# Splitting every second weight unit again in each batch, with its sign word from GpSimd and the last attention spread out

## The chip, the cores and the metric

The kernel runs on one core of one Trainium2 chip. The metric is device time in microseconds (us) of one execution. Five engines work side by side, each through its own queue in order: TensorE (PE, with its weight loads as PEld), VectorE (DVE), ScalarE (ACT), GpSimd (POOL) and SyncE (SP, which issues nearly all DMAs here).

## The reference

Attention with a soft cap, then a gated feed-forward layer, for 4 batches of 448 tokens, 12 heads of 64, a width of 768 and a hidden width of 1536:

```
scores = q k^T / sqrt(64);  scores = cap * tanh(scores / cap);  attn = softmax(scores);  a = attn v
x = a, laid out as [4*448, 768]
out = (sigmoid(x w_gate) * (x w_val)) w_out
```

q, k and v are float32. The three weight matrices are float64.

## The kernel before, in words

**Two streams on TensorE.** The attention works on 24 pairs of heads, six pairs to a batch. The feed-forward part, `moe(b)`, works on batch b. Both are Python generators, and the loop at the end of `_emit` weaves them: while `moe(b)` runs, the attention of batch b + 1 is issued in between. Each yields the size of the step it has issued, in TensorE terms, and the loop (L981) takes the attention's next step whenever `done_a * tot_m <= done_m * tot_a`, with `tot_m` 545 and `tot_a` = 12 x `o.head(b + 1)`. The instructions of TensorE and ScalarE keep the order in which they are issued here. The order of VectorE, GpSimd and SyncE is set by a planner when the kernel is built, from expected costs and from priorities (`high_priority`). [...]

**The feed-forward part.** The weights are cut into 36 units of 128 x 768: 24 for gate and value (an even unit and the odd one behind it belong together), 12 for the output. Each float32 operand is split into a high part (`o.hi`, a copy into fp32r) and a low part (`o.lo`, the difference), and each product is three fp32r matmuls: 18 of them by 448 columns for a gate or value unit (L836), 18 of 384 columns for an output unit in batches 0 to 2 (L927). A batch yields 24 x 18 = 432 steps for gate and value, and 12 x 3 x 5.14 = 185 for the output, 617 in all.

**The weights in batch 0.** A unit comes as 64-bit words into `w64` (three buffers). `convert_w` makes float32 words of it in one of two slots of `pair0`: ScalarE scales the upper words (L728), VectorE shifts them left by 3 (L729), ors in the sign bit of the upper word (L730), and adds the rounded lower word (L731). `split_w` splits the float32 unit into a tile of the pool `w` (four buffers), by ScalarE and VectorE (GpSimd for the first four units, which are converted before the feed-forward part begins). The split unit, 768 KB, is stored to DRAM (`store_w`, L777). `next_w(u)` converts up to unit u + 4, splits unit u + 3 and loads up to unit u + 3. The batches 1 to 3 load every unit split (`load_to`, L787).

**The attention of the pairs 12 to 23** (batches 2 and 3) splits its probabilities too. For a pair n and a head j: scores and tanh, exp, `emit_P` (ScalarE makes `ph`, VectorE `pl`; one buffer each), `emit_PV` (seven matmuls into the one PSUM bank `pv`, L459 to L461), `emit_rd` (ScalarE copies half of `pv` to `tmp`, L486, and VectorE adds it into `xraw`, L488, which frees `pv`). `emit_out` divides by the sum, and `x_done` splits the result into `xspl`. `emit_PV(n - 1, ...)` is issued in iteration n, between the scores of pair n. Iteration 24 has no scores of its own (`live` is false): only both `emit_PV` of pair 23 and its end are left.

Of the kernel before, what the change touches and what calls it, by code (L numbers as in the profile page):

```python
# [9 lines left out]
F32 = mybir.dt.float32  # L10
# [6 lines left out]
ALU = mybir.AluOpType  # L17
AX = mybir.AxisListType

P = 128  # L20
# [228 lines left out]
def _bounded_attention(o, x_done):  # L249
# [14 lines left out]
    nc, c, ap = o.nc, o.c, o.ap  # L264
# [3 lines left out]
    B, H, S, D, NF, NC, R = o.B, o.H, o.S, o.D, o.NF, o.NC, o.REST  # L268
# [6 lines left out]
    def direct(n):  # L275
        return n < DIRECT

    def alone(n):

        return n < o.NPAIR  # L280
# [3 lines left out]
    def held(n):  # L284

        return n < o.NPAIR - 1
# [6 lines left out]

        return 3 * AHEAD_OF if n == o.NPAIR - 1 else AHEAD_OF

    o.head = lambda b: 25 if direct(b * o.NPAIR) else 18.5


    fill = o.ps_m.tile([P, P], F32, tag="m", name="fill")
# [1 line left out]
    def keep_busy(n):  # L301

        for _ in range(n):
            nc.tensor.matmul(fill, ident, ident, start=True, stop=True)
# [97 lines left out]
    def emit_P(n, j):  # L402

        t = Pt[n][:, j]
        ph = ap.tile([P, NC, S], F32R, tag="ph", bufs=1, name=f"ph{n}_{j}")
        pl = ap.tile([P, NF, S], F32R, tag="pl", bufs=1, name=f"pl{n}_{j}")
        o.hi("a", ph, t)
        o.lo("v", pl, t[:, 0:NF, :], ph[:, 0:NF, :])
        o.lo("v", ph[R:P, NF, :], t[R:P, NF, :], ph[R:P, NF, :])
        Phl[n, j] = (ph, pl)  # L410
        a = ap.tile([P, S], F32, tag="a", bufs=1, name=f"a{n}_{j}")
        nc.gpsimd.tensor_add(a, t[:, 0, :], t[:, 1, :])  # L412
        nc.gpsimd.tensor_add(a, a, t[:, 2, :])
        nc.gpsimd.tensor_add(a[0:R], a[0:R], t[0:R, NF, :])
        f = a[0:D]
        nc.vector.tensor_add(f, f, a[D:P])
        s = ap.tile([P, S], F32R, tag="as", bufs=2, name=f"as{n}_{j}")
        o.hi("p", s[0:D], f)
        o.lo("v", s[D:P], f, s[0:D])
        Asum[n, j] = s  # L420
# [9 lines left out]
    def emit_R(n):  # L430

        for j in range(2):
            rows = half(j)
            nc.tensor.matmul(
                new_pv(n, j), vs[n][rows, NF, :], Pt[n][rows, 0, NF, :], start=True, stop=False
            )
# [89 lines left out]
    for n in range(NP + 1):  # L526
        live, last = n < NP, n == o.NPAIR
        if live:
            due = emit_S(n, 0) + emit_S(n, 1)
            if n in PLAN:  # L530
                o.convert_to(PLAN[n])
            yield due
        if n == 0:
            keep_busy(3)
        if n > 0:
            if packed(n - 1):
                emit_R(n - 1)
                yield 4
            yield from emit_PV(n - 1, 0)
            if not held(n - 1):  # L540
                emit_rd(n - 1, 0)
            if not direct(n - 1):
                emit_P(n - 1, 1)
        first = n == o.NPAIR
        if first:
            yield from emit_PV(n - 1, 1)
            emit_rd(n - 1, 1)
            emit_out(n - 1)
        if live:
            if packed(n):  # L550
                yield emit_S(n, 3) + emit_S(n, 2)
            else:
                yield emit_S(n, 2) + emit_S(n, 3)
            if n == 0:
                keep_busy(3)
            emit_T(n + 1)
            if n == 0:
                keep_busy(8)
            if 0 < n and n + 2 < NP:
                qks[n + 2] = o.load_qk(n + 2, direct(n + 2), packed(n + 2))  # L560
            yield 5
            if first:
                yield None
            emit_exp(n, 0)
            if not direct(n):
                emit_P(n, 0)
        if n > 0:
            if not first:
                yield from emit_PV(n - 1, 1)
                if alone(n - 1):  # L570
                    emit_rd(n - 1, 0)
                emit_rd(n - 1, 1)
                emit_out(n - 1)
                yield 2
            vs.pop(n - 1)
            if n % o.NPAIR == 0 and not first:
                yield None
            load_v(n + 1)
        if not live:
            return  # L580
        emit_exp(n, 1)
        split_v(n + 1)
# [84 lines left out]
def _emit(tc, ctx, c, attention_of, q, k, v, w_gate, w_val, w_out, out):  # L667
    nc = tc.nc
    B, H, S, D = q.shape
# [7 lines left out]
    WRAW = 2  # L677
    KEEP = 4
    AHEAD = 3
    WB = 4  # L680
    CLOSE = 3

    big = ctx.enter_context(tc.tile_pool(name="big", bufs=1))
    wp = ctx.enter_context(tc.tile_pool(name="wp", bufs=2))
    dram = ctx.enter_context(tc.tile_pool(name="dram", bufs=1, space=bass.MemoryType.DRAM))
    ps_m = ctx.enter_context(tc.tile_pool(name="ps_m", bufs=3, space=bass.MemoryType.PSUM))
    o = _Ops(tc, ctx, c, q, k, v)
# [7 lines left out]
    UN = KD * P  # L695
    NU = 3 * KF
# [7 lines left out]
            src.append(wt[:, x:x + KU])  # L704
    w_dram = {}
    w_raw = {}
    w_in = {}

    def load_w64(u):
# [4 lines left out]
    def convert_w(u):  # L714

        words = w_in.pop(u).bitcast(I32).rearrange("p (n t) -> p n t", t=2)
        low, top = words[:, :, 0], words[:, :, 1]
        at = conv["next"] % WRAW * UN
        x = c["pair0"][:, at:at + UN]
        xi = x.bitcast(I32)
        half = x.bitcast(U16).rearrange("p (n t) -> p n t", t=2)[:, :, 0]
        nc.scalar.activation(x, top.bitcast(F32), AF.Copy, scale=2.0 ** -112)  # L728
        nc.vector.tensor_scalar(xi, xi, 3, None, ALU.logical_shift_left)  # L729
        nc.vector.scalar_tensor_tensor(xi, top, -2 ** 31, xi, ALU.bitwise_and, ALU.bitwise_or)  # L730
        nc.vector.scalar_tensor_tensor(  # L731
            half, low.bitcast(U32), 2.0 ** -29, half, ALU.mult, ALU.add
        )
        w_raw[u] = x
        if u < o.early:
            split_w(u)

# [24 lines left out]
    def split_w(u):  # L762

        if u not in w_raw:
            return
        t, s = w_raw.pop(u), new_w(u)
        o.hi("p" if u < o.early else "a", s[:, 0, :], t)
        o.lo("p" if u < o.early else "v", s[:, 1, :], t, s[:, 0, :])
        if u < KEEP or u >= o.early:
            w_spl[u] = s  # L770
        if not u < KEEP:
            store_w(u, s)

    def store_w(u, s, queue=nc.sync):
# [1 line left out]
        w_dram[u] = d  # L776
        queue.dma_start(out=d.bitcast(F32), in_=s.bitcast(F32))  # L777

    loaded = {"next": 0}

    def load_to(n):
        while loaded["next"] < min(n, B * NU):
            u = loaded["next"]
            loaded["next"] += 1
            if KEEP <= u < o.early or NU <= u:
                t = new_w(u)
                nc.sync.dma_start(out=t.bitcast(F32), in_=w_dram[u % NU].bitcast(F32))  # L787
                w_spl[u] = t
# [24 lines left out]
    LEAD = 5  # L813
# [5 lines left out]
    def next_w(u):  # L819
        if u < NU:  # L820
            convert_to(u + LEAD)
        split_w(u + AHEAD)
        load_to(u + WB)
        w = w_spl.pop(u)
        if u < KEEP:
            store_w(u, w, nc.scalar)
        return w

    def moe(b):
# [75 lines left out]
        for t in range(2):  # L905
# [6 lines left out]
            end = b == B - 1 and t == 1  # L912
            by_chunk = KF - CLOSE * KU if end else KF
            x = 0
# [53 lines left out]
    with tc.manual_schedule(engines=MS):  # L968
# [4 lines left out]
        for b in range(B):  # L973
# [6 lines left out]
            while live_m or live_a:  # L980
                if live_a and (not live_m or done_a * tot_m <= done_m * tot_a):  # L981
                    n = next(att, None)
# [4 lines left out]
                else:  # L987
                    n = next(m, None)
# [34 lines left out]
```

## Time and profile before

| | |
|---|---|
| median of 3 runs | 759.17 us (758.65 to 760.04) |
| the profiled execution | 758.98 us |
| its span, first to last instruction | 757.2 us |
| PE busy | 742.8 us (98%) |
| PEld, DVE, ACT, POOL busy | 642.5, 467.4, 349.4, 202.3 us |
| granted TensorE clock, mean | 0.999 |
| DMA | 170.63 MB, mean 225 GB/s |

Busy times are sums over the whole span. The kernel has stages with different loads (attention alone, batch 0 with the conversions, batches 1 and 2 with attention, batch 3 without), so shares of the whole span say little of any one of them. A wait of an engine costs time only if the end hangs on that engine.

### The profile page before, as it was taken

What the parts mean: (1) busy time and instruction counts of PE and PEld (TensorE: products, weight loads), DVE (VectorE), ACT (ScalarE), POOL (GpSimd) and SP (SyncE); (2) the same over time, 40 slices, a digit from 0 to 9 for tenths busy, and PEclk for the clock granted to TensorE, in tenths of its full rate; (3) what the DMA queues carried; (4) which work ended last, traced back from release to release, by engine and by line L of the source; (5) the groups of instructions that cost most, each with busy time, mean ns of one, the idle gap of its engine ahead of it and who ended that gap; (6) DMA issues with size and microseconds to landing.
All of it is one profiled execution on the core that took longest, in us unless ns stands there. A gap on an engine that the chain in (4) does not pass through costs nothing.

```text
span 757.2 us, 10267 instructions
## 1 busy us (share of the span) xinstructions
PE 742.8 (98%) x3922; PEld 642.5 (85%) x3922; DVE 467.4 (62%) x503; ACT 349.4 (46%) x383; POOL 202.3 (27%) x223
## 2 busy tenths in 40 slices
PE   8999999999999999999999999999999999999997
PEld 7555878777778888988899988888889999999996
DVE  2698789979998938878786628878785011111000
ACT  5888577667576445555554245555540000000000
POOL 1354000021210516363535306353551000000000
PEclk9999999999999999999999999999999999999999
DMA  4867899999999866555677956644589866665541
GB/s 100 222 161 156 284 346 360 330 307 302 285 267 376 298 212 196 179 186 178 183 222 232 288 185 193 199 143 158 166 234 313 273 223 226 226 225 180 176 168 56
DMA packets 133509, 170.63 MB, mean 225 GB/s; under 512 B 86860, under 2 KB 111948, under 8 KB 133452
## 3 DMA queue, kind: packets, MB, share of 16 engines
q1 hardware_dynamic: 131788, 166.44, 69.8%
q10 hardware_dynamic: 1664, 3.46, 1.3%
q8 instruction: 33, 0.54, 0.3%
q14 instruction: 24, 0.20, 0.1%
HBM read 132.91 MB, written 36.18 MB: 223 GB/s over the span
## 4 chain that ended last, share of the span: by engine, by line
PE 78%; DVE 10%; DMA 3%; SPq 2%; issue 2%; POOL 2%; ACT 2%; DVEq 0%; POOLq 0%; ACTq 0%
PE h L836 43%; PE o L927 18%; PE sc L389 5%; PE pv L450 4%; DVE rd L506 2%; PE pv L459 2%; PE pv L460 2%; DVE pl L213 1%; PE tp L242 1%; DMA v<-in_v_dram 1%; PE pv L441 1%; DVE pair L731 1%; PE tp L350 1%; DVE pair L730 1%; DVE wspl L213 1%
## 5 line engine op out<-in xcount | busy, mean ns | idle before, releaser
L836 PE MATMUL h<-xspl,wspl 128*128 128x448 f32 x1728 | 377.4, 372 | 0.3 <-DVE osb L949 0.3
L836 PEld LDWEIGHTS h<-xspl,wspl 128*128 128x128 f32 x1728 | 321.3, 188 | 42.4 <-issue 15.5
L927 PE MATMUL o<-wspl,gspl 128*128 128x384 f32 x864 | 159.3, 338 | 0.2 <-DVE osb L949 0.2
L927 PEld LDWEIGHTS o<-wspl,gspl 128*128 128x128 f32 x864 | 150.5, 188 | 4.8 <-issue 3.8
L392 ACT ACTIVATE t<-sc,scale 128x896 f32<-128x896 f32 (+1 forms) x90 | 85.9, 1002 | 43.9 <-PE sc L389 43.7
L205 POOL TENSOR_SCALAR gspl<-gate 128x448 fp32r<-128x448 f32 x48 | 35.9, 748 | 251.7 <-DVE gate L880 251.7
L877 ACT ACTIVATE gate<-h 128x448 f32<-128x448 f32 x48 | 26.0, 541 | 161.3 <-PE h L836 159.8
L400 ACT ACTIVATE t<-t,capv 128x1792 f32<-128x1792 f32 (+2 forms) x48 | 83.2, 1738 | 0.1
L880 DVE SCALAR_TENSOR_TENSOR gate<-gate,h 128x448 f32<-128x448 f32 x48 | 29.7, 618 | 77.1 <-PE h L836 72.1
L506 DVE RECIPROCAL rd<-rd 128x448 f32<-128x448 f32 x24 | 70.7, 2946 | 5.3 <-ACT rd L479 3.1
L389 PE MATMUL sc<-T 64*128 64x448 f32 (+1 forms) x540 | 69.1, 382 | 1.9 <-DVE T L213 1.7
L389 PEld LDWEIGHTS sc<-T 64*128 64x128 f32 (+1 forms) x540 | 46.4, 181 | 22.3 <-issue 10.9
L949 DVE TENSOR_SCALAR osb<-o 128x384 f32<-128x384 f32 x22 | 12.0, 553 | 73.1 <-PE o L927 73.0
L412 POOL TENSOR_TENSOR a<-t 128x448 f32<-128x448 f32 x24 | 31.6, 1315 | 84.8 <-ACT t L400 46.9
L213 DVE TENSOR_TENSOR gspl<-gate,gspl 128x448 fp32r<-128x448 f32 x48 | 36.6, 763 | 22.3 <-POOL gspl L205 22.1
L207 ACT ACTIVATE ph<-t 128x1792 fp32r<-128x1792 f32 x24 | 40.7, 1696 | 16.4 <-PE pv L461 10.1
L213 DVE TENSOR_TENSOR pl<-t,ph 128x1344 fp32r<-128x1344 f32 x24 | 45.6, 1899 | 2.4 <-ACT ph L207 1.9
L213 DVE TENSOR_TENSOR T<-tp,T 128x960 fp32r<-128x960 f32 (+1 forms) x24 | 27.3, 1136 | 27.8 <-ACT T L207 27.8
L731 DVE SCALAR_TENSOR_TENSOR pair<-w,pair 128x768 uint16<-128x768 uint32 x36 | 41.7, 1162 | 0.3
L728 ACT ACTIVATE pair<-w 128x768 f32<-128x768 f32 x36 | 32.5, 904 | 18.9 <-DVE wspl L213 7.2
L450 PE MATMUL pv<-t,vo 112*128 112x448 f32 x96 | 40.1, 539 | 0.4 <-ACT t L400 0.4
L730 DVE SCALAR_TENSOR_TENSOR pair<-w,pair 128x768 int32<-128x768 int32 x36 | 35.5, 990 | 0.6
(81 smaller groups left out, 716.3 us busy)
## 6 DMA issues: line engine op xcount, KB each, us to landing
wspl<-wd SPq DMA_DIRECT2D x108, 768.0 KB, 4.4
wd<-wspl SPq DMA_DIRECT2D x32, 768.0 KB, 6.3
w<-in_moe_w_gate_dram SPq DMA_DIRECT2D x12, 768.0 KB, 6.7
w<-in_moe_w_val_dram SPq DMA_DIRECT2D x12, 768.0 KB, 7.0
w<-in_moe_w_out_dram SPq DMA_DIRECT2D x12, 768.0 KB, 7.1
qk<-in_q_dram SPq DMA_DIRECT2D x46, 112.0 KB, 4.1
out_dram<-osb SPq DMA_DIRECT2D x24, 192.0 KB, 3.3
qk<-in_k_dram SPq DMA_DIRECT2D x34, 96.0 KB, 2.7
```

The lines of the kernel that those rows point to most:

```text
L205: self.nc.gpsimd.tensor_scalar(dst, src, 1.0, 1.0, ALU.mult, ALU.mult)
L207: self.nc.scalar.activation(dst, src, AF.Copy)
L213: e.tensor_sub(dst, src, hi.bitcast(F32))
L389: nc.tensor.matmul(ps[0:w, j, 0:S], a[rows], r[rows], start=(i == 0), stop=(i == len(ops) - 1))
L392: nc.scalar.activation(Pt[n][0:w, :, m, :], ps[0:w, :, 0:S], AF.Tanh, scale=c["scale"][0:w])
L400: nc.scalar.activation(t, t, AF.Exp, scale=c["cap"][rows])
L450: nc.tensor.matmul(pv, vs[n][0:QC, j * NC + m, :], Pt[n][0:QC, j, m, :], start=(m == 0), stop=(m == NC - 1),)
L506: nc.vector.reciprocal(rd, rd)
L730: nc.vector.scalar_tensor_tensor(xi, top, -2 ** 31, xi, ALU.bitwise_and, ALU.bitwise_or)
L731: nc.vector.scalar_tensor_tensor(half, low.bitcast(U32), 2.0 ** -29, half, ALU.mult, ALU.add)
L836: nc.tensor.matmul(ps, a, r, start=(kk == 0 and i == 0), stop=(kk == KD - 1 and i == 2))
L927: nc.tensor.matmul(ps, a, r, start=(y + kk == 0 and i == 0), stop=(y + kk == KF - 1 and i == 2),)
```

## The change

Three things change.

**Sign word.** In `convert_w`, GpSimd multiplies the upper words by 0.0 in place, which leaves a word with the sign bit alone. One VectorE instruction then shifts and ors. L729 goes, L730 changes its form, and each conversion has a GpSimd instruction between ScalarE and VectorE.

**Units stored unsplit.** Of the units 4 to 27 the odd ones (12 of them) are stored as float32, 384 KB, straight from the slot of `pair0`, and not as split tiles. In the batches 1 to 3 they are loaded into the two slots of `pair0` by `load_raw_to`, up to unit u + 6 in `next_w(u)`, and `split_w` splits unit u + 3 by ScalarE and VectorE.

**The last attention.** `o.head` of batch 3 is 17.8 in place of 18.5, and iteration 24 yields 5 steps ahead of each of its two `emit_PV`.

```
-    o.head = lambda b: 25 if direct(b * o.NPAIR) else 18.5
+    o.head = lambda b: 25 if direct(b * o.NPAIR) else 17.8 if b == B - 1 else 18.5
...
+        if not live:
+            yield 5
         if n > 0:
             if packed(n - 1):
...
+        if not live:
+            yield 5
         if n > 0:
             if not first:
                 yield from emit_PV(n - 1, 1)
...
+    WHOLE = 28
...
+    def whole(u):
+        u %= NU
+        return u % 2 == 1 and KEEP <= u < WHOLE and o.early == KEEP
...
         nc.scalar.activation(x, top.bitcast(F32), AF.Copy, scale=2.0 ** -112)
-        nc.vector.tensor_scalar(xi, xi, 3, None, ALU.logical_shift_left)
-        nc.vector.scalar_tensor_tensor(xi, top, -2 ** 31, xi, ALU.bitwise_and, ALU.bitwise_or)
+        sign = top.bitcast(F32)
+        nc.gpsimd.tensor_scalar(sign, sign, 0.0, None, ALU.mult)
+        nc.vector.scalar_tensor_tensor(xi, xi, 3, top, ALU.logical_shift_left, ALU.bitwise_or)
...
         w_raw[u] = x
+        if whole(u):
+            d = dram.tile([P, UN], F32, name=f"wr{u}")
+            w_dram[u] = d
+            nc.sync.dma_start(out=d, in_=x)
...
-        if not u < KEEP:
+        if KEEP <= u < NU and not whole(u):
             store_w(u, s)
...
+    def load_raw_to(n):
+        while loaded["raw"] < min(n, B * NU):
+            u = loaded["raw"]
+            loaded["raw"] += 1
+            if NU <= u and whole(u):
+                at = loaded["slot"] % WRAW * UN
+                loaded["slot"] += 1
+                x = c["pair0"][:, at:at + UN]
+                nc.sync.dma_start(out=x, in_=w_dram[u % NU])
+                w_raw[u] = x
...
-            if KEEP <= u < o.early or NU <= u:
+            if KEEP <= u < o.early or NU <= u and not whole(u):
...
         load_to(u + WB)
+        load_raw_to(u + LEAD + 2)
```

## Rows read from the trace of the kernel before

**Rows 1.** Windows: the stretch, its length, busy us (instructions) by engine, clock, DMA.

```profile
120.00:140.00 20.00, 20.00 (x98) 16.00 (x97) 17.59 (x24) 13.35 (x17) 1.66 (x3) 1.00 1.07 361
...
480.00:500.00 20.00, 20.00 (x108) 17.49 (x107) 18.00 (x17) 11.74 (x13) 10.88 (x11) 1.00 0.56 181
...
560.00:580.00 20.00, 17.54 (x96) 16.64 (x95) 16.30 (x17) 5.44 (x6) 7.54 (x7) 1.00 0.93 258
```

**Rows 2.** Waits of PE, whole span: us in total, times, longest.

```profile
PE sc L389 <- DVE T L213: 1.7, 4, 0.7
```

**Rows 3.** Timeline of PE, in batch 0, then iteration 24: start, us, what, [idle before <- releaser].

```profile
214.57 0.66 PE L350 MATMUL tp<-ident,qk 128*128 128x128 f32 x4 [0.90 <-ACT t L392]
...
556.67 3.29 PE L927 MATMUL o<-wspl,gspl 128*128 128x384 f32 x18
...
562.40 0.44 PE L459 MATMUL pv<-pl,vs 128*128 128x448 f32 x1 [0.99 <-DVE xraw L488]
...
563.90 3.31 PE L927 MATMUL o<-wspl,gspl 128*128 128x384 f32 x18
568.69 0.47 PE L459 MATMUL pv<-pl,vs 128*128 128x448 f32 x1 [1.48 <-DVE pl L213]
```

**Rows 4.** The chain that ended last, behind iteration 24: start, us, what.

```profile
573.93 26.01 PE o L927 x150
```

**Rows 5.** Timeline of DVE, iteration 24.

```profile
561.64 0.61 DVE L488 TENSOR_TENSOR xraw<-pv,tmp 64x448 f32<-64x448 f32 x1
...
567.09 1.54 DVE L213 TENSOR_TENSOR pl<-t,ph 128x1344 fp32r<-128x1344 f32 x1
...
579.65 0.61 DVE L213 TENSOR_TENSOR xspl<-xraw,xspl 128x448 fp32r<-128x448 f32 x1
```

**Rows 6.** Groups by line: shapes xcount | busy us, mean ns | idle before.

```profile
L730 DVE SCALAR_TENSOR_TENSOR pair<-w,pair 128x768 int32<-128x768 int32 x36 | 35.5, 990 | 0.6
...
L213 DVE TENSOR_TENSOR wspl<-pair,wspl 128x768 fp32r<-128x768 f32 x32 | 32.8, 1024 | 0.7 <-ACT wspl L207 0.6
...
L207 ACT ACTIVATE wspl<-pair 128x768 fp32r<-128x768 f32 x32 | 27.0, 843 | 18.9 <-PE h L836 11.2 <-PE o L927 4.3 <-DVE pair L731 1.8
...
L729 DVE TENSOR_SCALAR pair<-pair 128x768 int32<-128x768 int32 x36 | 21.5, 596 | 14.6 <-ACT pair L728 14.5
...
L205 POOL TENSOR_SCALAR wspl<-pair 128x768 fp32r<-128x768 f32 x4 | 3.3, 832 | 4.0 <-DVE pair L731 4.0
```

**Rows 7.** Timeline of POOL ahead of batch 0: beside a conversion, and without one.

```profile
50.67 0.93 POOL L205 TENSOR_SCALAR xspl<-xraw 128x448 fp32r<-128x448 f32 x1 [3.26 <-DVE xraw L510]
51.68 1.71 POOL L213 TENSOR_TENSOR xspl<-xraw,xspl 128x448 fp32r<-128x448 f32 x1
...
70.78 1.13 POOL L213 TENSOR_TENSOR xspl<-xraw,xspl 128x448 fp32r<-128x448 f32 x1
```

**Rows 8.** Timeline of DVE, a tight place while batch 2's feed-forward runs.

```profile
473.67 1.54 DVE L213 TENSOR_TENSOR pl<-t,ph 128x1344 fp32r<-128x1344 f32 x1
```

**Rows 9.** PE's use of that tile.

```profile
478.16 0.36 PE L459 MATMUL pv<-pl,vs 128*128 128x448 f32 x1
```

**Rows 10.** DVE and its slot of `pair0` in batch 0.

```profile
127.00 1.05 DVE L731 SCALAR_TENSOR_TENSOR pair<-w,pair 128x768 uint16<-128x768 uint32 x1
```

**Rows 11.** ACT in batch 0: the slot's next use; a held split.

```profile
134.43 0.89 ACT L728 ACTIVATE pair<-w 128x768 f32<-128x768 f32 x1
...
211.65 0.85 ACT L207 ACTIVATE wspl<-pair 128x768 fp32r<-128x768 f32 x1 [3.03 <-PE o L927]
```

**Rows 12.** DMA issues: xcount, KB each, median us to landing.

```profile
wd<-wspl SPq DMA_DIRECT2D x32, 768.0 KB, 6.3
```

**Rows 13.** Timeline of DVE in the conversion of rows 7.

```profile
51.21 1.19 DVE L730 SCALAR_TENSOR_TENSOR pair<-w,pair 128x768 int32<-128x768 int32 x1
52.44 1.88 DVE L731 SCALAR_TENSOR_TENSOR pair<-w,pair 128x768 uint16<-128x768 uint32 x1
54.19 1.16 DVE L213 TENSOR_TENSOR T<-tp,T 128x960 fp32r<-128x960 f32 x1
```

More of the change, by code (lines that the diff above doesn't have):

```diff
@@ L777, in store_w @@
         queue.dma_start(out=d.bitcast(F32), in_=s.bitcast(F32))
-    loaded = {"next": 0}
+    loaded = {"next": 0, "raw": 0, "slot": 0}
+    def load_raw_to(n):
[8 more added lines that the diff above has]
+                w_raw[u] = x
     def load_to(n):
```

## The prediction, made before the changed kernel had run

> **What bounds the kernel now.** I read the busy time in stretches first, then PE's waits, then the timelines around each wait. In the stretches [rows 1] the reader sees a kernel bound by TensorE: in batch 0 (the first row) and while batch 2's feed-forward runs (the second) PE is busy for 20.00 of 20 us. An engine that gets less work there, or a queue that moves fewer bytes, gives nothing back by itself. One stretch late in the run falls short, 560 to 580 us with 17.54 busy: 2.46 us are missing. Two smaller places come from PE's waits: 1.7 us in four waits of scores for the low half of `T`, made by DVE, ahead of batch 0 [rows 2], and 0.90 us of a transpose for a tanh of ACT, at 214.57 in batch 0's output part [rows 3]. So the change can win at most about 2.5 + 1.7 + 0.9 us, unless it makes matmuls faster, which it doesn't touch.
>
> The hole is iteration 24, where the last pair has no scores left to stand between its two `emit_PV` [rows 3]. The first PV matmul at 562.40 has waited 0.99 us for `xraw` (L488 frees the bank `pv`), and that of the second head at 568.69 has waited 1.48 us for `pl`.
>
> **The spread of the last attention.** The two waits fall if the steps put between fill them. With the new `tot_a` of 12 x 17.8 = 213.6, five attention steps stand against 5 x 545 / 213.6 = 12.8 feed-forward steps, 2.5 chunks of 5.14, so two or three chunks. A chunk is six matmuls, 1.04 us by the chain's 150 in 26.01 us [rows 4]. So each yield puts 2.1 to 3.1 us of other TensorE work ahead of a PV.
>
> First wait: from the end of the previous PV (556.67, where the next matmuls start) to the end of L488 at 561.64 + 0.61 = 562.25 [rows 3, 5] are 5.6 us. The order left 562.40 - 0.99 - 556.67 = 4.7 us of work between; now 6.8 to 7.8. The wait goes, with at least 1.2 us to spare. Second wait: from 563.90 to the end of `pl` at 567.09 + 1.54 = 568.63 are 4.7 us, and 3.3 us of work stood between [rows 3, 5]; now 5.4 to 6.4, so at least 0.7 us to spare. Both together give 2.47 us.
>
> What is late next? The attention of batch 3 ends later, and batch 3 must find its `xspl`. Before, the attention's yields in this loop (five pairs of 37 steps and 16 at the end) came to 201 of 222, which ends it at 201 / 222 x 545 = 493 of the 617 feed-forward steps; now 211 of 213.6, at 538. That leaves (617 - 538) / 185 x 216 = 92 matmuls, 16 us by the same chain, in place of 26. The work behind the last yield is a normalization and a split of one row block, which ended at 580.26 [rows 5], 6.3 us into those 26 (they begin at 573.93). So some 10 us of cover are left. The last wspl splits of batch 3's units that `next_w` issues in the output part are those of units 25 and 27, issued with units 22 and 24, before iteration 24; none falls into it.
>
> **The sign word.** Per conversion DVE loses L729, 0.596 us, and the merged instruction should cost what L730 does, 0.990 (it has the same two inputs) [rows 6]. Over 36 units DVE gets 21.5 us less. GpSimd gets 36 instructions; the trace has none on every second word, so I bound them: nothing below, since it could hide fully, 0.83 us for a copy of as many packed words [rows 6], and 1.71 us, a subtraction beside a busy DVE [rows 7]. I take 0.83, the same count of elements, 30 us in all, in a stretch where GpSimd is busy 1.66 of 20 us [rows 1]. The chain of a conversion grows by 0.83 - 0.60 = 0.2 us. In batch 0 that is hidden twice: DVE's own time, and a lead of four units; if the cover were gone, it would cost 36 x 0.2 = 7 us at most. DVE's 21.5 us cover nothing that PE waits for, so they give zero, but for the 0.9 us and 1.7 us above, which I leave at zero: there the instruction that falls away is replaced by one that must be waited for.
>
> **Units stored unsplit.** Stores of 12 units shrink from 768 to 384 KB, and so do 36 loads: 48 x 0.384 MiB = 18 MiB less of 170.63 MB. PE waited for none of these loads, so this gives zero. In each later batch ACT gets 12 x 0.843 = 10.1 us and DVE 12 x 1.024 = 12.3 us [rows 6]. Two waits are new. On ACT the split of a unit waits for its load and for a buffer that TensorE frees with the unit before the current one; behind it stand the tanh and exp that are issued during the current unit, and TensorE reaches those no earlier. On SP a raw load waits until the slot's former unit is split, and behind it stand the loads of split units; these are issued three units ahead of their use, at least 3 x 3.3 us of output matmuls [rows 3], and a delay of some 3 us is covered. In batch 3 ACT and DVE are nearly idle. In batches 1 and 2 DVE is at up to 18.00 of 20 us [rows 1]; a whole unit comes every two units, some 10 us, so two a stretch, 2.0 us: 20.0. That is full in this stretch, so the slack decides. The tightest place of the PV chain is `pl`, ready at 473.67 + 1.54 = 475.21 and used at 478.16 [rows 8, 9], 2.95 us; three more of the 24 places are within 0.3 us of it. One split put into that chain delays it by 0.84 + 1.02 = 1.9 us, less than 2.95. I take zero; two splits at each of the four places would cost about 4 x (3.7 - 2.95) = 3 us, a split slowed by GpSimd to 1.8 us as many as four.
>
> The raw store holds the slot that the conversion two units later needs. In batch 0, L731 ends at 128.05 [rows 10] and the slot is used again at 134.43 [rows 11]: 6.4 us. A 768 KB store lands 6.3 us after its issue [rows 12]; half of it should land between 3.2 and 6.3. Unless SP's queue adds much, it fits, and I take zero.
>
> **Sum.** 758.98 (profiled) - 2.47 = 756.5. The median of the runs shown is 0.2 above the profiled execution, so 756.7.
>
> **Rivals.**
>
> *A wait in place of the one removed, no change.* The second PV has 0.7 us to spare only, and the pace of the whole last attention shifts by 4%. If DVE's order in iteration 24 puts 2 us of other work ahead of `pl`, most of the second wait comes back: 758.2 with all of it. Against it: the PV comes 2 us later, and the other work that stood there does not. With small delays elsewhere this is 757.7 to 760.6.
>
> *Held slots, slower.* SP's queue works in order; a raw store behind loads that wait can land later than 134.43. Then L728 stands at the head of ACT, and behind it the tanh that frees the score banks. The price is in the trace: a split that held ACT for 3.03 us, to 211.65 [rows 11], stands ahead of the tanh for which PE waited 0.90 us [rows 3]. Half of the 12 stores late by that much cost 6 x 0.9 = 5.4 us: 762.1. It decides from three such holds, which eat the gain; five make it slower.
>
> *GpSimd ahead of batch 0, slower.* There the low half of `T` stands behind the conversion on DVE, and PE waits for it. GpSimd begins the two instructions of a split of `xspl` at 50.67 [rows 7], beside the conversion. If the planner puts the sign word behind both, it starts at 53.4 and ends at 54.2, where the split of `T` now begins [rows 13], and the two VectorE instructions of the conversion come behind it: 0.99 to 1.19 and 1.05 to 1.88 [rows 6, 10, 13], 2.0 to 3.1 us. As DVE would stand idle meanwhile, the subtraction on GpSimd would take 1.13 in place of 1.71 [rows 7], so 1.4 to 3.1 us, in four conversions: 5.6 to 12.4 us, 762.3 to 769.1. It decides from a delay of 1 us each. Against it: GpSimd had stood idle for 3.26 us before that split [rows 7], waiting for DVE, and a sign word that the planner expects in this time goes first; then L730 and all behind it begin where they do now. The nearer end is the lower one. The Trainium skill (SBUF — State Buffer, "Who interferes with whom") has a VectorE instruction with two SBUF inputs and a GpSimd instruction that reads SBUF exclude each other. The trace agrees: L731 takes 1.88 us beside that subtraction and 1.05 without [rows 10, 13]. By that rule the sign word and these two instructions take turns, and the price would be near the upper end.
>
> *VectorE full in batches 1 and 2:* 3 to 4 us as worked out, 760.7.
>
> *More than the hole.* If both smaller waits go as well, 754.1.
>
> **How the numbers follow.** Chances: the forecast 0.50; more than the hole 0.07; no change 0.18; held slots 0.13; GpSimd ahead of batch 0 0.08; full VectorE 0.04, which lies at the bound and is halved. A measurement of this kernel can tell about 0.2%, 1.5 us, from no change. Faster: 0.50 + 0.07 = 0.57. Within: 0.18 + 0.02 = 0.20. Slower: 0.13 + 0.08 + 0.02 = 0.23. The likeliest case by itself has 755.5 to 757.6. The range goes from 754.8, which cuts the extra case, to 762.2, which takes in half of the held slots and leaves out what is worse.
>
> **What the profile would show.** Right: PE busy near 20 of 20 in the stretch of iteration 24, no wait of L459 for `xraw` or `pl`, some 92 output matmuls behind the attention in place of 150; DVE less busy by 15 to 21 us in batch 0 and more by 12 in each later batch; PE still full there. Wrong: waits of ACT's L728 for the raw store, waits of `sc` for `T` longer than 0.7 us before 75 us, waits of L459 in batches 1 and 2, or a wait at the start of batch 3.

## The result, and the profile of the changed kernel

The changed kernel takes 768.18 us (median of 4 executions, 766.60 to 770.98), the kernel before 759.22 beside it: a ratio of 1.0121 with a 95% interval of 1.0102 to 1.0139. It is 9 us slower, outside the range of the prediction. The profiled execution is the one of 770.98 us, so its trace shows some 3 us more loss than the median.

The groups by line come first. The line numbers have moved: L739 is the scaling by ScalarE (L728 before), L741 the sign word, L742 and L743 the two VectorE instructions of a conversion.

```profile
L741 POOL TENSOR_SCALAR w<-w 128x768 f32<-128x768 f32 x36 | 87.0, 2418 | 78.0 <-ACT pair L739 42.0 <-issue 28.9 <-DMA w<-in_moe_w_gate_dram 6.1
...
L213 DVE TENSOR_TENSOR wspl<-pair,wspl 128x768 fp32r<-128x768 f32 x68 | 74.1, 1090 | 24.5 <-ACT wspl L207 24.1
...
L207 ACT ACTIVATE wspl<-pair 128x768 fp32r<-128x768 f32 x68 | 57.4, 844 | 113.3 <-PE h L864 68.8 <-DVE pair L743 36.9 <-DMA wd<-wspl 4.5
...
L742 DVE SCALAR_TENSOR_TENSOR pair<-pair,w 128x768 int32<-128x768 int32 x36 | 38.2, 1061 | 12.8 <-POOL w L741 12.8
```

The sign word takes 2418 ns, not the 830 of the copy in [rows 6]. ACT's splits now wait 36.9 us for the end of a conversion; in [rows 6] it was 1.8. PE's waits, over the whole span:

```profile
PE sc L389 <- DVE T L213: 5.2, 4, 2.0
PE h L864 <- DVE osb L977: 2.9, 1, 2.9
PE tp L350 <- ACT t L392: 2.5, 2, 1.7
PE tp L242 <- ACT t L392: 2.3, 3, 1.0
...
PE o L955 <- DVE gate L908: 1.2, 1, 1.2
```

The first row stood at 1.7 us with a longest wait of 0.7 [rows 2]. The waits of L459 for `xraw` and `pl` [rows 3] are gone.

**Ahead of batch 0.** The same conversion as in [rows 7, 13], on POOL, then DVE, then PE:

```profile
53.41 2.27 POOL L741 TENSOR_SCALAR w<-w 128x768 f32<-128x768 f32 x1 [3.16 <-ACT pair L739]
55.61 0.59 POOL L205 TENSOR_SCALAR xspl<-xraw 128x448 fp32r<-128x448 f32 x1
56.28 1.72 POOL L213 TENSOR_TENSOR xspl<-xraw,xspl 128x448 fp32r<-128x448 f32 x1
```

```profile
55.71 1.29 DVE L742 SCALAR_TENSOR_TENSOR pair<-pair,w 128x768 int32<-128x768 int32 x1 [2.12 <-POOL w L741]
57.04 1.85 DVE L743 SCALAR_TENSOR_TENSOR pair<-w,pair 128x768 uint16<-128x768 uint32 x1
58.78 1.14 DVE L213 TENSOR_TENSOR T<-tp,T 128x960 fp32r<-128x960 f32 x1
```

```profile
37.61 1.96 PE L389 MATMUL sc<-T 64*128 64x448 f32 x10 [1.97 <-DVE T L213]
...
59.98 1.30 PE L389 MATMUL sc<-T 64*128 64x448 f32 x10 [1.97 <-DVE T L213]
...
272.07 1.49 PE L389 MATMUL sc<-T 64*128 64x448 f32 x12
276.48 6.74 PE L864 MATMUL h<-xspl,wspl 128*128 128x448 f32 x24 [2.92 <-DVE osb L977]
```

The sign word goes first on GpSimd, ahead of the split of `xspl`. DVE stands idle for 2.12 us, everything behind it follows later, the low half of `T` is late, and PE waits 1.97 us. Of the four such waits the longest was 0.7 us before.

**Half clock behind a wait.** The windows, with the granted clock in the third field from the right:

```profile
36.00:42.00 6.00, 4.39 (x16) 2.58 (x17) 5.80 (x6) 4.32 (x5) 3.65 (x4) 0.72 0.81 211
42.00:48.00 6.00, 6.00 (x28) 3.47 (x26) 4.63 (x4) 3.51 (x4) 4.86 (x5) 1.00 0.25 54
272.00:278.00 6.00, 3.08 (x18) 2.42 (x18) 4.76 (x7) 1.91 (x2) 5.01 (x5) 0.91 0.97 367
278.00:284.00 6.00, 6.00 (x26) 5.42 (x25) 1.24 (x2) 0.54 (x1) 0.73 (x2) 0.81 0.85 249
```

After the waits that end at 37.61 and 276.48 the clock falls from 2.4 to 1.2 GHz for a time. The windows give the price: 6 x 0.28 = 1.7 us in the first window, 6 x (0.09 + 0.19) = 1.7 in the last two. The rows show it too: ten matmuls of `sc` take 1.96 us at 37.61 and 1.30 at 59.98, behind a wait as long, with the clock at 1.00.

**Where the time went.** I set the start of the same matmul in both traces side by side. The changed kernel is 4.9 us behind when batch 0 begins (74 us; 0.6 of it is there from the start), 9.4 at 263 us, and 13.6 behind the boundary at 277. It stays at 13.6 to 547 us, wins 1.7 around iteration 24, and ends 11.9 behind. But for that 0.6, all of the loss lies where weights are converted; the batches 1 and 2, with 24 more splits, lose nothing. Between 74 and 263 us the 4.5 us go in steps of 0.2 to 1.1, nearly all of them where TensorE waits for a tanh (L392) or an exp (L400) of ACT.

**Iteration 24** is as forecast. PE's timeline, and the chain behind it:

```profile
571.08 2.35 PE L955 MATMUL o<-wspl,gspl 128*128 128x384 f32 x12 [1.24 <-DVE gate L908]
...
574.71 3.29 PE L955 MATMUL o<-wspl,gspl 128*128 128x384 f32 x18
...
578.24 4.33 PE L955 MATMUL o<-wspl,gspl 128*128 128x384 f32 x24
...
582.41 0.36 PE L459 MATMUL pv<-pl,vs 128*128 128x448 f32 x1
...
583.85 6.41 PE L955 MATMUL o<-wspl,gspl 128*128 128x384 f32 x36
590.10 0.36 PE L459 MATMUL pv<-pl,vs 128*128 128x448 f32 x1
```

```profile
595.23 16.64 PE o L955 x96
```

The 24 and the 36 matmuls stand ahead of the two `emit_PV`, which wait for nothing; 96 are left behind. One wait of 1.24 us for `gate` is new, just ahead.

### The profile page after: what moved, and what is told of

The parts are those of the page before. It is cut to its first block, busy times and chain, and to the rows that moved or that the text cites. A ratio compares the mean times of both kernels' runs of the same rounds, so it can differ in the third digit from the quotient of the medians.

```text
span 769.2 us, 10387 instructions
## 1 busy us (share of the span) xinstructions
PE 746.9 (97%) x3922; PEld 645.1 (84%) x3922; DVE 498.7 (65%) x503; ACT 379.2 (49%) x419; POOL 292.3 (38%) x259
## 2 busy tenths in 40 slices
DMA packets 133511, 151.78 MB, mean 197 GB/s; under 512 B 86860, under 2 KB 111948, under 8 KB 133452
## 4 chain that ended last, share of the span: by engine, by line
PE 75%; DVE 8%; DMA 5%; ACT 4%; POOL 2%; issue 2%; SPq 1%; ACTq 0%; DVEq 0%; POOLq 0%
PE h L864 39%; PE o L955 20%; PE sc L389 6%; PE pv L450 3%; DVE pair L743 2%; DMA wd<-wspl 2%; PE pv L460 2%; PE pv L459 2%; ACT t L392 2%; DVE pair L742 1%; POOL w L741 1%; DVE rd L506 1%; PE tp L242 1%; DMA w<-in_moe_w_gate_dram 1%; PE pv L441 1%
## 5 line engine op out<-in xcount | busy, mean ns | idle before, releaser
L741 POOL TENSOR_SCALAR w<-w 128x768 f32<-128x768 f32 x36 | 87.0, 2418 | 78.0 <-ACT pair L739 42.0
L207 ACT ACTIVATE wspl<-pair 128x768 fp32r<-128x768 f32 x68 | 57.4, 844 | 113.3 <-PE h L864 68.8
L392 ACT ACTIVATE t<-sc,scale 128x896 f32<-128x896 f32 (+1 forms) x90 | 86.0, 1002 | 29.7 <-PE sc L389 29.3
L205 POOL TENSOR_SCALAR gspl<-gate 128x448 fp32r<-128x448 f32 x48 | 34.1, 711 | 158.8 <-DVE gate L908 158.2
L213 DVE TENSOR_TENSOR wspl<-pair,wspl 128x768 fp32r<-128x768 f32 x68 | 74.1, 1090 | 24.5 <-ACT wspl L207 24.1
L400 ACT ACTIVATE t<-t,capv 128x1792 f32<-128x1792 f32 (+2 forms) x48 | 83.2, 1737 | 0.1
L977 DVE TENSOR_SCALAR osb<-o 128x384 f32<-128x384 f32 x22 | 11.9, 554 | 61.6 <-PE o L955 61.5
L743 DVE SCALAR_TENSOR_TENSOR pair<-w,pair 128x768 uint16<-128x768 uint32 x36 | 46.5, 1292 | 0.6
L742 DVE SCALAR_TENSOR_TENSOR pair<-pair,w 128x768 int32<-128x768 int32 x36 | 38.2, 1061 | 12.8 <-POOL w L741 12.8
L213 DVE TENSOR_TENSOR gspl<-gate,gspl 128x448 fp32r<-128x448 f32 x48 | 40.9, 852 | 7.6 <-POOL gspl L205 7.4
```

What stands on the lines that cost most here:

```text
L205: self.nc.gpsimd.tensor_scalar(dst, src, 1.0, 1.0, ALU.mult, ALU.mult)
L207: self.nc.scalar.activation(dst, src, AF.Copy)
L213: e.tensor_sub(dst, src, hi.bitcast(F32))
L392: nc.scalar.activation(Pt[n][0:w, :, m, :], ps[0:w, :, 0:S], AF.Tanh, scale=c["scale"][0:w])
L400: nc.scalar.activation(t, t, AF.Exp, scale=c["cap"][rows])
L741: nc.gpsimd.tensor_scalar(sign, sign, 0.0, None, ALU.mult)
```

## The experiments

The theory after this result: the length of the sign word on GpSimd carries the loss. The rival: the units stored unsplit carry it, by their stores, loads and 36 splits. "Before" is the kernel before, beside each group of runs (758.75 to 759.59 us).

**The parts alone.** First the change without its sign word:

```
-        sign = top.bitcast(F32)
-        nc.gpsimd.tensor_scalar(sign, sign, 0.0, None, ALU.mult)
-        nc.vector.scalar_tensor_tensor(xi, xi, 3, top, ALU.logical_shift_left, ALU.bitwise_or)
+        nc.vector.tensor_scalar(xi, xi, 3, None, ALU.logical_shift_left)
+        nc.vector.scalar_tensor_tensor(xi, top, -2 ** 31, xi, ALU.bitwise_and, ALU.bitwise_or)
```

> The changed kernel with the sign word made by VectorE as before (both its instructions back). Theory A (the whole loss comes from GpSimd's sign word, which takes 2.3 us where 0.83 was assumed, and the rest of the change gains 1.5 to 2.5 us): 756.5 to 758 us, no wait of the scores for T longer than 0.7 us. Theory B (the units stored unsplit cost, by held slots or by the splits of each batch): 762 to 768 us.

Measured: 757.64 us, 0.9982 [0.9973, 0.9991]. Without the sign word the change wins a little. Its price beside the rest is 768.18 - 757.64 = 10.5 us. Then the kernel before with the sign word alone; of the rest of the change nothing:

```
-        nc.vector.tensor_scalar(xi, xi, 3, None, ALU.logical_shift_left)
-        nc.vector.scalar_tensor_tensor(xi, top, -2 ** 31, xi, ALU.bitwise_and, ALU.bitwise_or)
+        sign = top.bitcast(F32)
+        nc.gpsimd.tensor_scalar(sign, sign, 0.0, None, ALU.mult)
+        nc.vector.scalar_tensor_tensor(xi, xi, 3, top, ALU.logical_shift_left, ALU.bitwise_or)
```

> The kernel before with the sign word alone. Theory A: 769 to 772 us, that is the changed kernel's 768.2 without what the spread of the last attention gave; the hole in iteration 24 of some 2.5 us is there again. Theory B: 758.5 to 762 us.

764.32 us, 1.0075 [1.0059, 1.0091], between both expectations: alone it costs 5.6 us, about half of what it costs in the whole. Then the kernel before with the spread of the last attention alone:

```
-    o.head = lambda b: 25 if direct(b * o.NPAIR) else 18.5
+    o.head = lambda b: 25 if direct(b * o.NPAIR) else 17.8 if b == B - 1 else 18.5
...
+        if not live:
+            yield 5
```

> The kernel before with the spread of the last attention alone. The prediction's own term: both waits of iteration 24 go, 2.47 us, so 756.5 to 757.2 us. Rival (the time lost there comes back in another place, as the wait of 1.2 us for the gate in the changed kernel's profile): 757.8 to 759.3 us.

756.90 us, 0.9967 [0.9954, 0.998]: by its median the fastest kernel of all. The ratio is worth 2.5 us (1.5 to 3.5 by its interval), the medians differ by 1.85, and the trace wins 2.6 around iteration 24; the forecast's term was 2.47. And the units stored unsplit alone (`whole`, `load_raw_to` and their calls, as in the change):

```
-        if not u < KEEP:
+        if KEEP <= u < NU and not whole(u):
             store_w(u, s)
...
+        load_raw_to(u + LEAD + 2)
```

> The kernel before with the units stored unsplit alone. Theory A: no change, 758.5 to 759.8 us, with the hole in iteration 24 as before. Theory B: 764 to 769 us.

762.96 us, 1.005 [1.0038, 1.0062]. This was missed, and it lies between the two expectations: alone they cost 4.2 us. The trace ends 3.5 us behind the kernel before; 3.0 of them are lost in iteration 24. DVE there, and PE's two waits:

```profile
556.27 0.95 DVE L213 TENSOR_TENSOR wspl<-pair,wspl 128x768 fp32r<-128x768 f32 x1
557.68 1.57 DVE L213 TENSOR_TENSOR gspl<-gate,gspl 128x448 fp32r<-128x448 f32 x1 [0.46 <-POOL gspl L205]
559.19 2.49 DVE L213 TENSOR_TENSOR pl<-t,ph 128x1344 fp32r<-128x1344 f32 x1
...
563.08 0.61 DVE L488 TENSOR_TENSOR xraw<-pv,tmp 64x448 f32<-64x448 f32 x1
```

```profile
563.84 0.44 PE L459 MATMUL pv<-pl,vs 128*128 128x448 f32 x1 [1.90 <-DVE xraw L488]
...
571.53 0.47 PE L459 MATMUL pv<-pl,vs 128*128 128x448 f32 x1 [1.32 <-DVE pl L213]
```

A split of a weight unit stands on DVE ahead of the chain that the last pair waits for, and that chain has no slack there: 1.90 us where [rows 3] has 0.99. Behind it the granted clock is 0.91 and 0.92 in the windows 556 to 566 and 566 to 576, 1.7 us of the 3.0. With the spread the PV matmuls come later, and most of that cost goes (757.64 with both against 756.90).

**Which property of the instruction is slow.** The conversions take five forms in turn on GpSimd: the change's (every second word, one operation), the same with two operations, one that reads packed words, and packed words in place with one operation and with two.

```
+        form = conv["next"] % 5
+        if form == 0:
             nc.gpsimd.tensor_scalar(sign, sign, 0.0, None, ALU.mult)
+        elif form == 1:
+            nc.gpsimd.tensor_scalar(sign, sign, 0.0, 1.0, ALU.mult, ALU.mult)
+        elif form == 2:
+            nc.gpsimd.tensor_scalar(sign, x, 0.0, 1.0, ALU.mult, ALU.mult)
+        elif form == 3:
+            nc.gpsimd.tensor_scalar(x, x, 1.0, None, ALU.mult)
+        else:
+            nc.gpsimd.tensor_scalar(x, x, 1.0, 1.0, ALU.mult, ALU.mult)
```

> The changed kernel with five forms of the GpSimd instruction by turns, seven or eight conversions each: (1) every second word in place, one operation, as in the change; (2) the same with two operations (times 0.0, times 1.0); (3) the packed float32 unit read, every second word written; (4) the packed unit in place, one operation; (5) the packed unit in place, two operations. In (4) and (5) it multiplies by 1.0 and VectorE makes the sign as before. Theory S (the step of two words makes it 2.3 us): (1) and (2) 2.2 to 2.3 us, (3) between, (4) and (5) about 0.83. Theory O (an instruction with one operation is the slow one): (1) and (4) 2.2 to 2.3 us, the others 0.8 to 1.0.

764.45 us in one execution. The groups of POOL, shapes kept apart, in the order of forms 0, 3, 4, 1, 2:

```profile
L743 POOL TENSOR_SCALAR w<-w 128x768 f32<-128x768 f32 x8 | 19.8, 2472 | 23.7 <-ACT pair L739 16.1 <-issue 7.6
...
L749 POOL TENSOR_SCALAR pair<-pair 128x768 f32<-128x768 f32 x7 | 17.2, 2451 | 18.2 <-ACT pair L739 18.2
...
L751 POOL TENSOR_SCALAR pair<-pair 128x768 f32<-128x768 f32 x7 | 7.1, 1014 | 14.9 <-ACT pair L739 14.9
...
L745 POOL TENSOR_SCALAR w<-w 128x768 f32<-128x768 f32 x7 | 6.7, 962 | 10.4 <-ACT pair L739 10.4
...
L747 POOL TENSOR_SCALAR w<-pair 128x768 f32<-128x768 f32 x7 | 6.4, 910 | 29.6 <-ACT pair L739 29.6
```

With one operation it takes 2.45 to 2.47 us, with two 0.91 to 1.01, and packed or not makes no difference. The instruction that does less arithmetic takes 2.5 times as long. So the change itself, with two operations:

```
-        nc.gpsimd.tensor_scalar(sign, sign, 0.0, None, ALU.mult)
+        nc.gpsimd.tensor_scalar(sign, sign, 0.0, 1.0, ALU.mult, ALU.mult)
```

> The whole change with one word more: GpSimd's instruction multiplies by 0.0 and by 1.0, two operations, in place on every second word. Theory O2 (the form with one operation is what made it slow, and the loss follows its length): the instruction at 0.9 to 1.0 us, the total at 757.5 to 761 us, and no waits of the scores for T longer than 0.8 us. Rival (the further hop over GpSimd costs, whatever its length): 764 to 768 us.

759.60 us, 1.0008 [0.9999, 1.0017]:

```profile
L741 POOL TENSOR_SCALAR w<-w 128x768 f32<-128x768 f32 x36 | 36.3, 1011 | 96.5 <-ACT pair L739 61.6 <-issue 30.3 <-DMA grest<-gspl 3.2
```

```profile
PE sc L389 <- DVE T L213: 1.8, 3, 0.6
```

One operand, `1.0`, takes back 768.18 - 759.60 = 8.6 of the 9 us (8.3 against the kernel before beside each). The waits for `T` are back at those of [rows 2], and no stretch at half clock is left. VectorE's order is the same in both kernels up to 78 us, so ahead of batch 0 it is the length that counts; in batch 0 the order differs at some 40 places too, and the length and that order are not told apart there.

**What the hop itself costs.** Two operations and the spread, without the units stored unsplit (against the change):

```
-        nc.gpsimd.tensor_scalar(sign, sign, 0.0, None, ALU.mult)
+        nc.gpsimd.tensor_scalar(sign, sign, 0.0, 1.0, ALU.mult, ALU.mult)
...
-        if whole(u):
-            d = dram.tile([P, UN], F32, name=f"wr{u}")
...
-        load_raw_to(u + LEAD + 2)
```

> Sign word with two operations and the spread, without unsplit units. The unsplit units cost 0.7 us beside the spread and the hop over GpSimd 2 us beside both (759.6 against 757.6); if the hop alone costs nothing without the unsplit units: 756.5 to 757.5 us; if it costs 2 us by itself: 758.3 to 759.5 us.

759.14 us, 1.0003 [0.9994, 1.0012]. This is the second expectation. Against the spread alone (756.90) a sign word of 1 us still costs some 2.2 us. Two neighbours of it: the same without the first two lines of that diff, so with the one-operation form, and the whole change with two operations that read packed words:

```
-        nc.gpsimd.tensor_scalar(sign, sign, 0.0, None, ALU.mult)
+        nc.gpsimd.tensor_scalar(sign, x, 0.0, 1.0, ALU.mult, ALU.mult)
```

> The sign word and the spread of the last attention, without the units stored unsplit. By the runs of the parts alone (+5.6 and -1.9) the sum is 762.5 us. Theory U (the unsplit units make the sign word dearer: 768.2 - 757.6 = 10.5 us with them against 5.6 alone): 761.5 to 763.5 us, and no stretch at half clock ahead of 700 us. Rival (the spread makes it dearer, or chance in the planner's order): 766 to 768.5 us.

> The whole change, with GpSimd reading the packed float32 unit in place of every second word, and two operations; it still writes every second word. If the instruction comes to 1.2 us or less and its length is what costs: 757.5 to 760.5 us. If it stays at 2 us or more: 766 to 769 us.

761.76 us, 1.0034 [1.0019, 1.0049], and 760.94 us, 1.0012 [1.0001, 1.0023]. The first is as expected. The second is 0.4 us above its nearer expectation, with an instruction of 0.97 us: the packed read brings nothing over 759.60. ScalarE in place of GpSimd (a copy with scale 0.0; the sign words, and with them the output, are not the reference's here):

```
-        nc.gpsimd.tensor_scalar(sign, sign, 0.0, None, ALU.mult)
+        nc.scalar.activation(sign, sign, AF.Copy, scale=0.0)
```

> The whole change, with the sign word made by ScalarE (copy with scale 0.0, some 0.9 us) behind its scaling, so that no engine but ScalarE stands between. Theory L (what costs is the length of the GpSimd instruction on the way to VectorE): 756.5 to 759 us. Rival (any further step of the conversion costs as much, whichever engine makes it, and ScalarE is needed for the attention): 762 to 768 us.

758.68 us, 0.9991 [0.9981, 1.0001], as the first theory expected: right behind the scaling on the same engine the step costs 1.0 us by the medians (757.64 without a sign word) and 0.2 against the kernel before beside each.

**Where the long sign word costs.** The first four units, converted ahead of batch 0, by VectorE as before, all others by GpSimd:

```
+        if u < o.early:
+            nc.vector.tensor_scalar(xi, xi, 3, None, ALU.logical_shift_left)
+            nc.vector.scalar_tensor_tensor(xi, top, -2 ** 31, xi, ALU.bitwise_and, ALU.bitwise_or)
+        else:
```

> The whole change, but the first four units, which are converted ahead of batch 0, get their sign from VectorE as before. If the scores' waits for T ahead of batch 0 cost what the profile of the change shows there (4.3 us, half of it by a stretch at half clock): 763 to 765 us. If the time would be lost later anyway: 766 to 768.5 us.

765.64 us, 1.0084 [1.0069, 1.01], between the two expectations: the place that the rival "GpSimd ahead of batch 0" named is worth 2.5 us of the loss, not most of it. Next, the sign word and the unsplit units without the spread:

```
-    o.head = lambda b: 25 if direct(b * o.NPAIR) else 17.8 if b == B - 1 else 18.5
+    o.head = lambda b: 25 if direct(b * o.NPAIR) else 18.5
...
-        if not live:
-            yield 5
```

> The sign word and the units stored unsplit, without the spread. By the parts alone the sum is 759.2 + 5.6 + 4.2 = 769 us. Theory U (the unsplit units make the slow sign word dearer also without the spread, by some 5 us): 772 to 775 us. Rival (only all three together are dearer): 767.5 to 770 us.

773.53 us, 1.0189 [1.0174, 1.0205], as the first theory expected: 14.6 us, where the two alone make 5.6 + 4.2 = 9.8. So the unsplit units make the long sign word dearer by some 5 us; beside the sign word of two operations they add only 759.60 - 759.14 = 0.5.

**Why the two make each other dearer.** First the units stored both ways in batch 0 and loaded split:

```
-            w_dram[u] = d
...
-        if KEEP <= u < NU and not whole(u):
+        if KEEP <= u < NU:
...
-            if KEEP <= u < o.early or NU <= u and not whole(u):
+            if KEEP <= u < o.early or NU <= u:
...
-        load_raw_to(u + LEAD + 2)
```

> The whole change, with the 12 units stored both ways and loaded split in all batches, so that only the store out of the slot is left of the unsplit units. If that store (by the slot or by SP's queue) makes the sign word dearer in batch 0: 766.5 to 769.5 us. If it is the missing split stores or the later loads and splits: 761.5 to 764 us, as for sign and spread alone (761.8).

772.76 us, 1.0169 [1.0147, 1.019], above both expectations. It is slow with nothing split in the later batches, but it adds 12 stores. ACT waited for them:

```profile
ACT pair L739 <- DMA wr<-pair: 8.3, 4, 3.0
```

That is the rival "held slots" of the prediction; in the changed kernel the same wait is 0.3 us. To keep the traffic out, two more kernels. One has batch 0's stores as before (all units stored split) and the later batches as changed, with the high halves of the stored units as loaded words; the other has batch 0 as changed and loads split units only, taking for an unsplit one the unit ahead of it, so its weights are wrong.

```
-                nc.sync.dma_start(out=x, in_=w_dram[u % NU])
+                nc.sync.dma_start(out=x, in_=w_dram[u % NU].bitcast(F32)[:, 0, :])
```

```
-                nc.sync.dma_start(out=t.bitcast(F32), in_=w_dram[u % NU].bitcast(F32))
+                nc.sync.dma_start(out=t.bitcast(F32), in_=w_dram[(u - 1 if whole(u) else u) % NU].bitcast(F32))
```

> The whole change, but batch 0 stores all 32 units split, as the kernel before does, with no store from the slots of pair0. The batches 1 to 3 are as in the change: 36 loads of 384 KB into the slots, 36 splits (the loaded words are the high halves of the stored units, so the output's low part is missing). The one-operation sign word stays. Theory S (the store out of the slot in batch 0 is what makes the slow sign word dearer): as sign word and spread together, 761.8 to 763, and ACT's waits for wspl L207 <- DVE pair between 80 and 275 us near 21 us. Theory L (the later batches' loads and splits do it): 766 to 769. Theory M (both halves are needed, or each bears a part): 764 to 766.

> The whole change, but the batches 1 to 3 load every unit split (in place of a unit stored unsplit, the split unit ahead of it is loaded, so these weights are the wrong ones), and nothing is split in them. Batch 0 is as in the change: 12 stores of 384 KB out of the slots of pair0, 20 of split units. No traffic is added beside the change's in batch 0, which the run that stored both ways did. Theory S: as the whole change, 766 to 769.5, with ACT's waits for wspl L207 <- DVE pair near 37 us. Theory L: 761.8 to 763. Theory M: 764 to 766.

764.70 us, 1.0067 [1.0044, 1.009], and 769.00 us, 1.0119 [1.0099, 1.0139]. The second is as slow as the whole change, as theory S has it. The first lies above the 761.8 to 763 of theory S, in the range of theory M; its trace has two stretches at half clock ahead of batch 0, which differs in nothing there from the run with sign word and spread, whose trace has none (6.0 and 2.8 us behind the kernel before at 74 us). From 74 to 277 us the first loses 1.7 us more, like sign word and spread (1.7); the second loses 7.3. In iteration 24 the first wins 1.6 us where sign word and spread win 2.7: there the later splits cost about 1 us, with the 1.2 us wait for `gate`. So in batch 0 it is the store, by the traces; the medians alone don't settle it. ACT's longest total in batch 0 (80 to 275 us), first kernel, then second:

```profile
ACT wspl L207 <- DVE pair L743: 19.3, 11, 5.1
```

```profile
ACT wspl L207 <- DVE pair L743: 33.2, 17, 5.1
```

DVE at the end of batch 0, again in this order:

```profile
271.72 0.56 DVE L973 TENSOR_SCALAR osb<-o 128x384 f32<-128x384 f32 x1
272.20 1.51 DVE L213 TENSOR_TENSOR xspl<-xraw,xspl 128x448 fp32r<-128x448 f32 x1
273.64 1.01 DVE L973 TENSOR_SCALAR osb<-o 128x384 f32<-128x384 f32 x2
```

```profile
273.86 1.54 DVE L213 TENSOR_TENSOR xspl<-xraw,xspl 128x448 fp32r<-128x448 f32 x1 [0.46 <-POOL xspl L205]
275.33 1.47 DVE L976 TENSOR_SCALAR osb<-o 128x384 f32<-128x384 f32 x3
```

The store out of the slot goes with another order of DVE. In the second kernel, as in the change, all three copies `osb` stand behind the split of `xspl`; in the first, one stands ahead. PE needs the first `osb` for its next bank: 2.9 us of waiting, and half clock behind it, against 1.1 and none. With the clock that is 3.6 of the 5.6 us between the two kernels. The order alone is not to blame, for the kernel before has it too (DVE, then PE):

```profile
262.35 1.56 DVE L213 TENSOR_TENSOR xspl<-xraw,xspl 128x448 fp32r<-128x448 f32 x1 [0.46 <-POOL xspl L205]
263.84 1.48 DVE L949 TENSOR_SCALAR osb<-o 128x384 f32<-128x384 f32 x3
```

```profile
264.44 3.77 PE L836 MATMUL h<-xspl,wspl 128*128 128x448 f32 x17 [0.32 <-DVE osb L949]
```

There DVE comes to the copies early enough, and in the change with two operations, which has this order too, PE waits 0.4 us; with the long sign word DVE is late, and then the order counts. The other 2.0 us are lost by 251 us, in three waits of transposes for ACT's tanh (0.84, 0.27 and 0.88 more than in the first kernel). The first two come before the orders of DVE or GpSimd differ (232 us), so another order is not their cause; what is stays open. A higher priority for that copy was to bring it ahead:

```
-                    with tc.high_priority(offset=2 * AHEAD_OF):
+                    with tc.high_priority(offset=(12 if b == 0 and t == 1 else 2) * AHEAD_OF):
```

> The whole change, with a higher priority for VectorE's three copies of the last output banks of batch 0, so that the planner may put them ahead of the division and the split that stand there. If their place makes the wait of 2.9 us and the stretch at half clock at the start of batch 1: 764 to 765 us, against 768.2. If they are late for another reason: 767 to 769 us.

769.28 us, 1.0138 [1.0122, 1.0154]. DVE's order at that place didn't change and the wait stayed at 2.9 us, so this run says nothing on the order.

**Can the small waits be won?** The spread alone, with the conversions ahead of batch 0 issued behind `emit_T`:

```
-            if n in PLAN:
-                o.convert_to(PLAN[n])
...
+            if n in PLAN:
+                o.convert_to(PLAN[n])
```

> The spread alone, and ahead of batch 0 each conversion issued behind the transposes of the next pair instead of before them, so that VectorE makes the low half of T first. If the scores' waits for T (1.7 us in four places) go: 755.2 to 756 us, against 756.9 for the spread alone. If the conversion comes too late for the first matmuls of batch 0, or DVE takes it first all the same: 756.5 to 758 us.

760.56 us (755.80 to 766.84), 1.0021 [0.9999, 1.0043], above both expectations. The waits for `T` fall to 0.5 us, and another takes their place:

```profile
PE tp L242 <- ACT t L392: 3.0, 1, 3.0
```

Behind it comes a stretch at half clock, at 76 us. No gain.

## Why the prediction was wrong

**The step that failed** is the price of the sign word: "I take 0.83, the same count of elements". The row it came from is a copy with two operations; the change's instruction has one. It measured 2.42 us, outside both bounds (0 and 1.71). The rows of the kernel before held no `tensor_scalar` of GpSimd with one operation, so the upper bound was not a bound. With two operations the same instruction takes 1.01 us, near the value taken, and the kernel comes to 759.60: 8.6 of the 9 us hang on this one instruction, by its length and by the order of VectorE that goes with it.

**Hidden, so taken at zero.** A conversion, from the start of the scaling to the end of the last VectorE instruction, took 5.65 us on average over the 36 before, 7.30 in the change and 6.00 with two operations (worked out from the timelines). So the chain grew by 1.65 and not by 0.2. The merged VectorE instruction is a small part of it: 1.06 us against the 0.99 taken. The lead of four units did hide most of 36 x 1.65 = 59 us. It hid nothing ahead of batch 0, where `T` stands behind the conversion on DVE, nor where ACT's split waits at the head of its queue for a conversion. Even at 1 us the hop costs some 2 us (759.14 against 756.90, 759.60 against 757.64); the forecast had none.

**What a stall costs.** I priced stalls by their length alone. Behind waits of 1.9 to 3 us the clock fell to half in many traces, 1.7 us each time. Two such stretches make 3.4 of the 11.9 us in the changed kernel's trace.

**The spread: right.** 7.7 us of work stand ahead of the first `emit_PV` (574.71 to 582.41) where 6.8 to 7.8 were forecast, 6.3 ahead of the second (583.85 to 590.10; 5.4 to 6.4 forecast), and 96 matmuls behind (92). Alone it brings 2.5 us by its ratio, 1.85 by the medians.

**Units stored unsplit at zero: right only beside the spread, and not for the reasons given.** "None falls into iteration 24" was wrong: alone, a split stands on DVE ahead of `pl` there, and 3.0 of the 3.5 us by which that trace is behind are lost there (4.2 us by the medians). Beside the spread 0.5 to 0.7 us are left; what the traces show in that place is the 1.2 us wait for `gate`. That the batches 1 and 2 have room was right. The traffic fell as forecast, from 170.63 to 151.78 MB, which is 18 MiB (384 KB are 0.375 MiB, not the 0.384 of the product). What the forecast lacked is that with the long sign word the store out of the slot costs some 5 us in batch 0: 3.6 of the 5.6 us measured lie where DVE's order differs, and the cause of the other 2.0 is open.

**The rivals.** "GpSimd ahead of batch 0" had the right place and a wrong reason: the sign word goes first, not behind the split of `xspl`, but is long. DVE stands idle 2.12 us where L729 took 0.6, and PE's wait at this conversion grew from 0.40 to 1.97, that is by 1.57. It made 2.5 of the 9 us. "Held slots" appeared only where a store was added (8.3 us); in the change it is 0.3. The Trainium skill's rule behind the first (SBUF — State Buffer, "Who interferes with whom") agrees with the trace, but decided nothing: L743 takes 1.85 us beside the subtraction on GpSimd, as L731 did [rows 13].

**Still open:** why a wait of the same length is followed by half clock at one time and not at another, as with the waits at 37.61 and 59.98 here, or with the 2.9 us for `osb`, which had none behind it in the run with the higher priority; what the planner's order at the end of batch 0 costs by itself; and how the store out of the slot makes ACT late before any order differs.

## What to carry to other kernels

Price an instruction that moves to another engine by a row with the same operation, number of operations and operands; an equal count of elements is not the same instruction, and the nearest row is a bound only if it is known to be the slower form. If no such row exists, put the forms side by side in one kernel first: one run settled here what the sum had missed. A step that leaves a chain for another engine costs where that chain has no lead, as ahead of batch 0 here, and a store that holds a buffer longer can go with another order, made from expected times, far from it.

## What the runs showed of the hardware

**One operation is slower than two on GpSimd.** `tensor_scalar` on 128x768 float32 took 2.42 us on average in the change with one operation, a multiplication (2.21 to 2.91), and 1.01 with a second one, a multiplication by 1.0. Other operations and types were not tried. The Trainium skill (GPSIMD Engine Reference, "3.1 Elementwise — side-by-side cycle accounting") counts 1.03 cycles per element "for k ≤ 2", which I read as a body of up to two operations. An estimate from that figure of the Trainium skill, at its 1.2 GHz, is 768 x 1.03 / 1.2 = 659 ns and a fixed part. The two-operation copy of 832 ns [rows 6] fits it, the one-operation form does not, and the measurement decides. With two operations a stride of two words made no difference that shows: 962 ns on average against 1014 packed, and 865 against 831 for the shortest.

**TensorE at half clock behind short waits.** Waits of 1.97 and 2.92 us were followed by stretches at 1.2 GHz that cost 1.7 us each, as the windows show. Much of the scatter between executions goes with how many of them one meets: the same kernel but for a priority, with none in its trace, took 766.09 us, the change with two 770.98, and 3.4 of these 4.9 us are the two stretches.
